# 64-row matmul pairs for the q, k, v products of a gated attention and MLP kernel

## The chip, the cores and the metric

The kernel runs on one core of a Trainium2 chip. The metric is device time in microseconds (us) for one execution of the whole program. A core has TensorE (matrix products, abbreviated PE), VectorE (DVE), ScalarE (ACT), GpSimd (POOL) and SyncE (SP), each with its own queue of instructions that it takes in order; in this kernel SP issues all DMA transfers. Engines wait for one another by semaphores. SBUF is the on-chip memory of 128 partitions ("rows" below). PSUM holds TensorE's results; this kernel uses it as eight tiles of 128 rows by 512 float32, four with the tag "m" and four with the tag "b", handed out in turn within each tag.

## The reference

Two branches read the same x of 2048 positions by 448 features and are mixed by a gate. All matrices are float32.

```
g   = sigmoid(sum(x * gate_w))                       # one number per position
qkv = x @ wqkv                                       # 448 -> 3 x 448, 16 heads of 28
a   = softmax over 8 positions (i, i-2, ... i-14) of q.k / sqrt(28), times v;  then @ wo
b   = relu(x @ w1 + b1)^2 @ w2 + b2                  # 448 -> 1792 -> 448
out = g * a + (1 - g) * b
```

## The kernel before

**Precision.** Every matrix product is made of one-pass products in the type fp32r. Each operand is split: ScalarE writes a rounded copy ("h", high), VectorE writes the rest ("l", low, float32 minus h). A product is then h·h + h·l + l·h. `split_full` (L99) is one such pair of instructions.

**Contraction.** 448 features are three blocks of 128 rows and a last one of 64. A full block takes three matmuls. The last block is stored twice, in rows 0 to 63 and 64 to 127: `x7` holds the high part of x in both halves, `x8` the low part, and `w7` the low part of the weights in rows 0 to 63 and the high part in rows 64 to 127 (`split_w7`, L103), so that two matmuls of 128 rows do it. `pairs` (L132) lists these 3 x 3 + 2 = 11 matmuls of a tile.

**Stage A, the q, k, v products (L447 to L497).** Positions are sorted into even and odd ones, since attention steps by two, and into four chunks c of 512. A chunk has four tiles of 128 positions. Each tile and each of q, k, v (b = 0, 1, 2) is one PSUM tile of 128 positions by 448 features (450 for q, whose last columns are the gate), so there are 4 x 4 x 3 = 48 PSUM tiles of 11 matmuls. Chunk 0 computes q and k with `qkv_wide` (L182), which goes block by block over four tiles because the operands are still arriving, and v tile by tile with `qkv_block` (L175). Chunks 1 to 3 take two tiles at a time: q, q, k, k, v, v, from the tags b, b, m, m, b, b and then m, m, b, b, m, m. ScalarE evacuates each finished tile to a staging tile in SBUF (`qkv_evacuate`, L167), and SP stores it to DRAM (q_d, k_d, v_d; L171), from where attention loads it in another layout.

**What stands between.** While a chunk is computed, the next chunk's x is loaded (`x_load`, L393, 1 MB), split by ScalarE and VectorE, and its split form is written to DRAM (`x_spill`, L128, eight transfers) for stage B. Quarters of w1 and halves of w2 are loaded and split as well (`w1_piece`, L373; `w2_piece`). All of these raw loads share two buffers. At most eight of SP's transfers are under way: each waits for the one eight places before it.

**Order.** The program order is written by hand. A planner keeps a clock of TensorE time: `advance(dt)` (L350) moves it by the cost of the matmuls just issued (`MM448` = 203 ns each), then issues what falls due: work that was put off with `at(dt, fn)`, and the next pieces of attention. The pieces of w1 and w2 are put off by times in `WEIGHTS` (L439), so their ScalarE copies stand between evacuations in ScalarE's queue.

**Attention** starts when the first half of the positions is in DRAM. GpSimd multiplies, VectorE reduces, each in order; it runs on beside the second half of stage A and most of stage B.

**Stage B (L678 to L712)** takes the chunks in the order 3, 0, 1, 2: the MLP, and between its steps the product with wo for the positions that attention has finished. An output tile gets two additions by VectorE, one from each branch (`fin_add`, L572). After the first, the half sum goes to DRAM (f_d, L578); before the second it is loaded again (L552), and the sum goes to `out` (L575). In the last chunk, c = 2 (par = 1, t = 0 to 3), the wo half comes first, and the MLP's half ends the program.

**The start.** Thirteen float32 matmuls of 128 columns on a tile of zeros (L403) run while the first weights and x arrive. The zeros' buffer has the tag "k" of the pool `attp`, and so has the raw copy of the k weights (L416), which is loaded once the warm-up is through with it. Gates are computed after chunks 1 and 3 (`gates`, L268): an exponential on ScalarE, then add, reciprocal and multiply-add on VectorE.

Of the kernel before, what the change touches and what calls it, by code (L numbers as in the profile page):

```python
# [19 lines left out]
G = 4  # L20
# [22 lines left out]
WARM = 13  # L43
PP_BUFS = 4
# [6 lines left out]
def gated_mix_kernel(ctx: ExitStack, tc: tile.TileContext, xT, wqkv, w1, w2, wo, b1, b2, out):  # L51
# [97 lines left out]
    wq7 = ap.tile([P, 3, NQ], F32R, name="wq7")  # L149
# [6 lines left out]
    def qkv_pairs(x, tl, b):  # L156
        n = NQ if b == 0 else D
        sl = slice(tl * P, tl * P + P)
        return n, pairs(lambda k: x.h[k][:, sl], lambda k: x.l[k][:, sl], x.x7[:, sl], x.x8[:, sl],
                        lambda k: wqh[:, k, b, :n], lambda k: wql[:, k, b, :n], wq7[:, b, :n])  # L160

    def qkv_evacuate(pt, c, tl, b):
        par, t = c // 2, (c % 2) * 4 + tl
        if t % 2 == 0:
            stage[b] = ap.tile([P, G, 2, C], F32, tag="stage", name=f"st{c}_{tl}_{b}", bufs=ST_BUFS)
        st = stage[b]
        nc.scalar.activation(st[:, :, t % 2], pt[:, :D].rearrange("p (g c) -> p g c", g=G), AF.Copy)  # L167
        if t % 2 == 1:
            dst, off = ((q_d, 0), (k_d, HALO), (v_d, HALO))[b]
            dd = dst[par, :, off:off + SP].rearrange("g (p s) c -> p g s c", s=NS)[:, :, t - 1:t + 1]  # L170
            nc.sync.dma_start(dd.rearrange("p g s c -> p g (s c)"), st.rearrange("p g s c -> p g (s c)"))  # L171
# [3 lines left out]
    def qkv_block(x, c, tl, b, tag):  # L175
        pt = ps(tag, f"qkv{c}_{tl}_{b}")
        n, pr = qkv_pairs(x, tl, b)
        for i, (a, w) in enumerate(pr):
            nc.tensor.matmul(pt[:, :n], a, w, start=i == 0, stop=i == len(pr) - 1)  # L179
        return lambda: qkv_evacuate(pt, c, tl, b)  # L180

    def qkv_wide(x, c, b, tag):  # L182

        pts = [ps(tag, f"qkv{c}_{tl}_{b}") for tl in range(4)]
        todo = [qkv_pairs(x, tl, b) for tl in range(4)]
        for lo, hi in ((0, 3), (3, 6), (6, 9), (9, 11)):
            for tl in range(4):
                n, pr = todo[tl]
                for i in range(lo, hi):
                    nc.tensor.matmul(pts[tl][:, :n], *pr[i], start=i == 0, stop=i == len(pr) - 1)  # L190
        return [lambda tl=tl: qkv_evacuate(pts[tl], c, tl, b) for tl in range(4)]
# [76 lines left out]
    def gates(par):  # L268
        e = smp.tile([P, NS], F32, tag="e", name=f"e{par}")
        nc.scalar.activation(e, zt[:, par], AF.Exp, scale=-1.0)  # L270
        nc.vector.tensor_scalar_add(e, e, 1.0)
        nc.vector.reciprocal(gt[:, par], e)
        nc.vector.tensor_scalar(g1t[:, par], gt[:, par], -1.0, 1.0, op0=ALU.mult, op1=ALU.add)
# [126 lines left out]
    zero = attp.tile([P, P], F32, tag="k", name="zero")  # L400
    nc.vector.memset(zero, 0.0)  # L401
    for _ in range(WARM):
        nc.tensor.matmul(warm[:, :P], zero, zero, start=True, stop=True)  # L403
# [4 lines left out]
    for k in range(4):  # L408
        nc.sync.dma_start(raws[0][:, k, :NQ], wqkv[0, :, k])
# [3 lines left out]
    raw3 = attp.tile([P, 2, D], F32, tag="q", name="wqraw_3")  # L413
    for b, tag in ((1, "k"), (2, "v")):
        raw = attp.tile([P, 3, D], F32, tag=tag, name=f"wqraw{b}")
        raw = [raw[:, k] for k in range(3)] + [raw3[:, b - 1]]  # L416
        for k in range(4):
            nc.sync.dma_start(raw[k], wqkv[b, :, k, :D])
        raws.append(raw)
    x = x_tiles(0, ap)  # L420
# [9 lines left out]
    split_w7(raws[0][:, 3, :NQ], wq7[:, 0])  # L430
    split_x78(rx[:, 3], x.x7, x.x8)

    def wq_split(b):
        for k in range(3):
            split_full(raws[b][k], wqh[:, k, b, :D], wql[:, k, b, :D])
        split_w7(raws[b][3], wq7[:, b, :D])
# [3 lines left out]
        (0, 8): [lambda: w1_piece(0, 3 * QT)],  # L440
        (1, 2): [lambda: w1_piece(1, 4 * QT)],
        (1, 8): [lambda: w1_piece(2, 3 * QT)],
        (2, 2): [lambda: w1_piece(3, 4 * QT)],
        (2, 8): [lambda: w2_piece(0, 4, w2ah, w2al, 0, 3 * QT)],
        (3, 2): [lambda: w2_piece(4, 3, w2ah, w2al, 0, 4 * QT)],
    }
    for c in range(4):  # L447
        if c == 0:
            order = [(0, None), (1, None)] + [(2, tl) for tl in range(4)]
        else:  # L450
            order = [(b, 2 * tp + i) for tp in range(2) for b in range(3) for i in range(2)]
        done = 0
        for b, tl in order:
            if done == 0 and c < 3:
                rx = x_load(c + 1)
            if done == 0 and c == 0:
                wq_split(1)
            if done == 4 and c == 0:
                wq_split(2)
# [5 lines left out]
            for piece in WEIGHTS.get((c, done), ()):  # L465
                piece()
            if done == (8 if c == 0 else 4) and c < 3:
                xn = x_tiles(c + 1, xpool if c % 2 == 0 else ap)
                x_split(rx, xn)
                if c + 1 < 3:  # L470
                    x_spill(c + 1, xn)
            if done == 4 and c == 0:
                x_spill(0, x)
            if tl is None:
                evs = qkv_wide(x, c, b, "bm"[b])
                for ev in evs:
                    advance(QT)
                    ev()
                done += 4
            else:  # L480
                ev = qkv_block(x, c, tl, b, "bm"[done // 2 % 2])
                advance(QT)
                ev()
# [271 lines left out]
```

## Time and profile before

| | |
|---|---|
| time, median of 3 runs | 442.14 us (441.98 to 446.45) |
| the profiled execution: its time | 442.13 us |
| its span, first to last instruction | 440.4 us |
| TensorE busy | 433.5 us, 2082 records |
| VectorE, ScalarE, GpSimd busy | 260.0, 178.5, 273.6 us |
| granted TensorE clock | 0.999 |
| DMA | 67.44 MB, mean 153 GB/s |
| warm-up matmuls (L403) | 1.06 to 6.69 us |
| q, k, v matmuls (L190, L179) | 6.69 to 114.58 us, 528 of them |

The profile is one execution on the chip. A row of a view in order of time gives the start in us, the duration in us, engine, line, operation, what is written and read, and in brackets how long the engine was idle before and what ended the wait. "PEld" is TensorE's loading of weights, which runs beside the matmuls. A line such as "SPq" is the issue of a transfer by SP's queue, not the transfer. The chain of work that ended last is followed back from the last instruction: at each step to what released it, or to the instruction before it on its engine. In the view by stage each row is a stretch of time: its length, then busy time and count for PE, PEld, DVE, ACT and POOL, then the granted clock, the busy share of the DMA engines and their GB/s.

### The profile page before, as it was taken

How to read it: one execution, taken by the hardware profiler on the slowest of the kernel's cores; microseconds unless marked ns; L12 is line 12 of the kernel's file. 1: busy time of each engine (PE TensorE's matmuls, PEld its weight loads, DVE VectorE, ACT ScalarE, POOL GpSimd, SP SyncE). 2: the span in 40 equal slices, each digit the busy share in tenths (PEclk: the TensorE clock that was granted, in tenths of full speed). 3: DMA queues.
4: the chain of work that ended last, by engine and by line, in shares of the span. 5: the costliest groups of instructions: out<-in, count | busy, mean ns of one | idle time of the engine just before them, and what ended most of it. 6: DMA issues, size and time to landing. Idle time of an engine off the chain costs nothing.

```text
span 440.4 us, 5662 instructions
## 1 busy us (share of the span) xinstructions
PE 433.5 (98%) x2082; PEld 385.8 (88%) x2082; DVE 260.0 (59%) x345; ACT 178.5 (41%) x367; POOL 273.6 (62%) x167
## 2 busy tenths in 40 slices
PE   9999999999999999999999999999999999999994
PEld 8999999999888888888888888888888888888994
DVE  4522411774799996666655857543857757653542
ACT  3644532643455433453334453234233333334520
POOL 1000003574999999999989997641899988690000
PEclk9999999999999999999999999999999999999999
DMA  7899979678560321821203754010544400100145
GB/s 227 323 309 378 384 227 345 238 229 293 172 247 6 136 105 40 309 98 44 78 1 120 237 180 151 34 41 22 173 151 154 173 1 0 78 1 0 64 156 200
DMA packets 37899, 67.44 MB, mean 153 GB/s; under 512 B 3184, under 2 KB 27888, under 8 KB 37488
## 3 DMA queue, kind: packets, MB, share of 16 engines
q1 hardware_dynamic: 37872, 67.08, 44.4%
q8 instruction: 16, 0.26, 0.2%
q14 instruction: 11, 0.09, 0.1%
HBM read 42.38 MB, written 24.69 MB: 152 GB/s over the span
## 4 chain that ended last, share of the span: by engine, by line
PE 97%; DMA 1%; DVE 0%; SPq 0%; DVEq 0%; issue 0%
PE h L533 32%; PE b L594 30%; PE qkv L179 20%; PE a L635 8%; PE qkv L190 4%; PE warm L403 1%; PE oT L612 1%; DMA bt<-f_d 1%; PE oT L613 0%; DVE bt L573 0%; SPq L552 0%; DVEq L750 0%; SPq L575 0%; DVE zero L401 0%; DVEq L573 0%
## 5 line engine op out<-in xcount | busy, mean ns | idle before, releaser
L226 POOL TENSOR_TENSOR qk<-q,k 128x896 f32<-128x896 f32 x64 | 137.8, 2183 | 102.4 <-DMA k<-k_d 71.6
L233 POOL TENSOR_TENSOR av<-lg,v 128x896 f32<-128x896 f32 x64 | 122.8, 2017 | 12.9 <-DVE o L239 6.6
L539 ACT ACTIVATE h<-h,b1t 128x512 f32<-128x512 f32 x56 | 37.1, 662 | 164.1 <-PE h L533 164.0
L179 PE MATMUL qkv<-wqh,x 128*128 128x448 f32 (+1 forms) x240 | 75.0, 367 | 0.0
L542 DVE TENSOR_TENSOR hl<-h,hh 128x512 fp32r<-128x512 f32 x56 | 38.5, 688 | 59.2 <-ACT h L541 59.0
L227 DVE TENSOR_REDUCE lg<-qk 128x32 f32<-128x896 f32 x64 | 67.1, 1076 | 4.0 <-POOL qk L226 4.0
L239 DVE TENSOR_REDUCE o<-av 128x112 f32<-128x896 f32 x64 | 66.7, 1075 | 2.1 <-POOL av L233 2.1
L179 PEld LDWEIGHTS qkv<-wqh,x 128*128 128x128 f32 x240 | 45.2, 188 | 3.8
L179 PE MATMUL qkv<-wql,x 128*128 128x448 f32 (+1 forms) x120 | 44.0, 366 | 0.0
L594 PE MATMUL b<-w2bh,hh 128*128 128x448 f32 x112 | 41.0, 366 | 0.0
L594 PE MATMUL b<-w2bl,hh 128*128 128x448 f32 x112 | 40.9, 366 | 0.0
L594 PE MATMUL b<-w2bh,hl 128*128 128x448 f32 x112 | 40.9, 365 | 0.0
L594 PE MATMUL b<-w2ah,hh 128*128 128x448 f32 x112 | 40.7, 364 | 0.0
L594 PE MATMUL b<-w2ah,hl 128*128 128x448 f32 x112 | 40.6, 362 | 0.0
L594 PE MATMUL b<-w2al,hh 128*128 128x448 f32 x112 | 40.5, 361 | 0.0
L167 ACT ACTIVATE st<-qkv 128x448 f32<-128x448 f32 x48 | 25.4, 547 | 23.3 <-PE qkv L179 17.3
L540 ACT ACTIVATE hh<-h 128x512 fp32r<-128x512 f32 x56 | 33.6, 600 | 1.8
L541 ACT ACTIVATE h<-h 128x512 f32<-128x512 f32 x56 | 33.2, 593 | 0.0
L533 PE MATMUL h<-x1b,w1h 128*128 128x512 f32 x84 | 28.6, 394 | 0.0
L533 PE MATMUL h<-x2b,w1h 128*128 128x512 f32 x84 | 28.5, 393 | 0.0
L533 PE MATMUL h<-x0b,w1h 128*128 128x512 f32 x84 | 28.4, 391 | 0.0
L533 PE MATMUL h<-x,w1h 128*128 128x512 f32 x84 | 28.2, 390 | 0.0
(104 smaller groups left out, 761.2 us busy)
## 6 DMA issues: line engine op xcount, KB each, us to landing
k<-k_d SPq DMA_DIRECT2D x8, 840.0 KB, 5.1
v<-v_d SPq DMA_DIRECT2D x8, 840.0 KB, 5.8
x_d<-x SPq DMA_DIRECT2D x24, 256.0 KB, 4.8
q_d<-st SPq DMA_DIRECT2D x8, 448.0 KB, 4.7
k_d<-st SPq DMA_DIRECT2D x8, 448.0 KB, 4.9
w1raw<-w SPq DMA_DIRECT2D x4, 896.0 KB, 9.1
v_d<-st SPq DMA_DIRECT2D x8, 448.0 KB, 4.4
q<-q_d SPq DMA_DIRECT2D x8, 448.0 KB, 3.4
```

What stands on the lines that cost most here:

```text
L179: nc.tensor.matmul(pt[:, :n], a, w, start=i == 0, stop=i == len(pr) - 1)
L226: nc.gpsimd.tensor_mul(pr, q[:, s:s + 1].to_broadcast([P, W, C]), k[:, s:s + W])
L227: pending.append(lambda: nc.vector.tensor_reduce(lg[:, s], pr.rearrange("p w (h d) -> p w h d", h=HG), axis=AX.X, op=ALU.add))
L233: nc.gpsimd.tensor_mul(pr.rearrange("p (h d) w -> p w h d", h=HG), lg[:, s][:, :, :, None].to_broadcast([P, W, HG, DH]), v[:, s:s + W].rea ...
L239: pending.append(lambda: nc.vector.tensor_reduce(o[:, g * C:(g + 1) * C], pr, axis=AX.X, op=ALU.add))
L533: nc.tensor.matmul(pt, w, a, start=i == 0, stop=i == len(pr) - 1)
L539: nc.scalar.activation(pt, pt, AF.Relu, bias=b1t[:, f:f + 1])
L540: nc.scalar.activation(hh, pt, AF.Square)
L541: nc.scalar.activation(pt, pt, AF.Square)
L542: at(HL_DELAY, lambda: nc.vector.tensor_sub(hl, pt, f32(hh)))
L594: nc.tensor.matmul(bps[tl][:, :D], a[:, sl], w, start=f == 0 and i == 0, stop=f == NF - 1 and i == 2)
L635: nc.tensor.matmul(pa[:, :D], a, w, start=i == 0, stop=i == len(pr) - 1)
```

## The change

**Pairs.** In stage A the contraction is cut into products of 64 rows. A PSUM tile now takes 21 of them: 9 full matmuls as two halves each, and three for the last 64 rows (h·h, h·l, l·h). `side_by_side` issues them in pairs: one product on rows 0 to 63 for one PSUM tile, one on rows 64 to 127 for another. Two tiles thus take 21 pairs instead of 22 matmuls. Each tile gets the products of one half of the rows first, and those of the other half later, beside another tile; the lists in `run`, `qkv_first` and `qkv_two` set this order, and `Acc` keeps count.

**Turns.** Between the two halves `turn` has VectorE write a zero into an unused column of the PSUM tile (ScalarE for two of them in chunk 0). This write waits for the matmuls of the first half, and those of the second wait for it. There are 44 such VectorE writes and 2 on ScalarE. In most cases nine pairs of other tiles are issued between a turn and the matmul that waits for it.

**Chunk 0** keeps 36 full q matmuls (three blocks, four tiles), with 2, 1 and 0 filler matmuls on the zeros after the blocks (`FILL`). Then come 48 pairs, which finish q and make k, and 42 for v. Chunks 1 to 3 have two parts of 63 pairs each, whose tiles have the tags m, m (q), m, b (k), b, b (v). Evacuations are issued at the pair after which a tile is done.

**Weights.** The last 64 rows of q's and k's weights share one tile (rows 0 to 63 and 64 to 127), split into `w7h` and `w7l`; v's stay doubled. One weight load of 224 KB is gone and one is cut into two.

**Order.** The split and the spill of the next x, and the pieces of w1 and w2, are put off to other planner times. The filler matmuls read the zeros too, so the load of the k weights, which takes their buffer, now waits for the last filler.

**Other parts.** Warm-up: fp32r, one pass, 256 columns, 13 matmuls as before. Gates: the addition and the multiply-add move from VectorE to ScalarE. Last output halves: `fin_add` keeps the half sums of par = 1, t < 4 in SBUF, so these four are neither stored to f_d nor loaded again.

The core of the diff:

```diff
+    def side_by_side(*todo):
+        for pair in zip(*todo):
+            for r, (acc, a, w) in enumerate(pair):
+                rows = slice(r * 64, r * 64 + 64)
+                nc.tensor.matmul(acc.pt[:, :acc.n], a[rows], w[rows], start=acc.todo == 21, stop=acc.todo == 1)
+                acc.todo, acc.rows = acc.todo - 1, r
+
+    def turn(one, two):
+        for acc in (one, two) if one is not two else (one,):
+            if one is two:
+                nc.scalar.activation(acc.pt[0:1, 511:512], ident[0:1, 1:2], AF.Copy)
+            else:
+                nc.vector.memset(acc.pt[0:1, 511:512], 0.0)
+            acc.rows = None
...
+    def last(x, acc, tl, b):
+        sl, n = slice(tl * P, tl * P + P), ncols(b)
+        h, l = w7h[:, b // 2, :n], w7l[:, b // 2, :n]
+        return [(acc, x.x7[:, sl], h), (acc, x.x7[:, sl], l), (acc, x.x8[:, sl], h)]
...
+    def run(c, todo, steps):
+        a = 0
+        for e, done, *turns in steps:
+            side_by_side(todo[0][a:e], todo[1][a:e])
+            while a < e:
+                advance(min(12, e - a) * MM448)
+                a = min(a + 12, e)
+            for one, two in turns:
+                turn(one, two)
+            for b, tl, acc in done:
+                qkv_evacuate(acc.pt, c, tl, b)
...
+        for k in range(3):
+            for i in four:
+                for j, (acc, a, w) in enumerate(full(x, q[i], i, 0, (k,))):
+                    nc.tensor.matmul(acc.pt[:, :NQ], a, w, start=k == j == 0, stop=False)
+            advance(12 * MM448)
+            for _ in range(FILL[k]):
+                nc.tensor.matmul(warm[:, :2 * P], zero[:, :P], zero, start=True, stop=True)
...
+    def qkv_two(x, c, t0):
+        t1 = t0 + 1
+        (q0, q1), (k0, k1), (v0, v1) = (accs(c, b, (t0, t1), tags) for b, tags in enumerate(("mm", "mb", "bb")))
+        run(c, [full(x, q0, t0, 0) + last(x, q0, t0, 0) + full(x, q1, t1, 0) + last(x, q1, t1, 0) + full(x, k0, t0, 1)
+                + full(x, k1, t1, 1) + full(x, v0, t0, 2) + last(x, v0, t0, 2) + full(x, v1, t1, 2),
+                full(x, k1, t1, 1) + last(x, k1, t1, 1) + full(x, v0, t0, 2) + full(x, v1, t1, 2) + last(x, v1, t1, 2)
+                + full(x, q0, t0, 0) + full(x, q1, t1, 0) + full(x, k0, t0, 1) + last(x, k0, t0, 1)],
+            [(24, [], (q0, k1)), (33, [], (q1, v0)), (42, [(0, t0, q0), (1, t1, k1)], (k0, v1)),
+             (51, [(0, t1, q1)]), (54, [(2, t0, v0)]), (63, [(1, t0, k0), (2, t1, v1)])])
...
-        nc.vector.tensor_scalar_add(e, e, 1.0)
+        nc.scalar.activation(e, e, AF.Copy, bias=1.0)
         nc.vector.reciprocal(gt[:, par], e)
-        nc.vector.tensor_scalar(g1t[:, par], gt[:, par], -1.0, 1.0, op0=ALU.mult, op1=ALU.add)
+        nc.scalar.activation(g1t[:, par], gt[:, par], AF.Copy, scale=-1.0, bias=1.0)
...
-    zero = attp.tile([P, P], F32, tag="k", name="zero")
+    zero = attp.tile([P, 2 * P], F32R, tag="k", name="zero")
...
-        nc.tensor.matmul(warm[:, :P], zero, zero, start=True, stop=True)
+        nc.tensor.matmul(warm[:, :2 * P], zero[:, :P], zero, start=True, stop=True)
...
+        (0, 2): lambda: w1_piece(0, 3 * QT),
+        (1, 0): lambda: w1_piece(1, 6 * QT),
+        (1, 1): lambda: w1_piece(2, 5 * QT),
+        (2, 0): lambda: w1_piece(3, 6 * QT),
+        (2, 1): lambda: w2_piece(0, 4, w2ah, w2al, 0, 5 * QT),
+        (3, 0): lambda: w2_piece(4, 3, w2ah, w2al, 0, 6 * QT),
...
+                at(4 * QT if c else 8 * QT + 25 * MM448, lambda c=c, rx=rx: x_next(c + 1, rx))
...
+        elif par == 1 and t < 4:
+            ahead[par, t] = bt
+            fin[par, t] = "half"
```

## The prediction

> **What bounds the kernel now.** I read four views in this order: busy time by engine, the chain of work that ended last (its start and, in a second answer, its end: start us, us, what), ScalarE's rows in order of time during the q, k, v products, and the busy time of the engines by stage.
>
> ```profile
> PE 433.5 (98%) x2082; PEld 385.8 (88%) x2082; DVE 260.0 (59%) x345; ACT 178.5 (41%) x367; POOL 273.6 (62%) x167
> ```
> ```profile
> 1.06 5.63 PE warm L403 x26
> 6.69 17.98 PE qkv L190 x88
> 24.67 89.91 PE qkv L179 x440
> ```
> ```profile
> 411.45 0.33 PE oT L612 x3
> 411.77 0.11 PE oT L613
> ...
> 431.81 3.74 DMA bt<-f_d
> ...
> 435.68 0.51 DVE bt L573
> ```
>
> TensorE is busy for 98% and is the chain nearly everywhere, so a matmul less is time less, as long as nothing else ends last. Two reserves show: 5.63 us of warm-up, and the end, where 3.74 us go to reloading a half output. The products fill 6.69 to 114.58 us: 528 matmuls, 107.89 / 528 = 0.2043 us each. The transposes show how fast TensorE goes when the streamed operand is short: 0.11 us for one matmul with its own weight load.
>
> ```profile
> 35.74 0.58 ACT L100 ACTIVATE w1h<-w1raw 128x448 fp32r<-128x448 f32 x1 [6.02 <-DMA w1raw<-w]
> 36.23 0.53 ACT L167 ACTIVATE st<-qkv 128x448 f32<-128x448 f32 x1
> ...
> 79.39 2.20 ACT L100 ACTIVATE x<-xraw 128x512 fp32r<-128x512 f32 x4 [9.19 <-DMA xraw<-xT]
> 81.50 0.52 ACT L167 ACTIVATE st<-qkv 128x448 f32<-128x448 f32 x1
> ```
> ```profile
> 6.70:15.70 9.00, 9.00 (x45) 8.30 (x45) 6.45 (x12) 5.31 (x12) 0.00 (x0) 1.00 1.01 354
> 15.70:24.70 9.00, 9.00 (x45) 8.31 (x45) 2.22 (x4) 3.98 (x11) 0.00 (x0) 1.00 0.74 259
> 24.70:33.70 9.00, 9.00 (x46) 8.32 (x46) 2.50 (x4) 3.69 (x8) 0.00 (x0) 1.00 1.00 329
> 33.70:60.60 26.90, 26.90 (x133) 24.78 (x132) 7.48 (x12) 11.83 (x28) 0.00 (x0) 1.00 1.05 373
> ```
>
> The last two columns are the DMA engines' busy share and GB/s: here they are full. ScalarE takes its work in order, and it twice stands for 6.02 and 9.19 us on a load, with evacuations of finished PSUM tiles (L167) queued behind. TensorE does not notice, because the next tiles it writes are ones emptied long before. That spare decides this change.
>
> **The pairs.** Chunk 0 keeps 36 full-height q matmuls, then has 48 + 42 pairs; chunks 1 to 3 have 126 pairs each. That is 36 + 468 = 504 slots for 528. At 0.2045 us a pair the 24 missing slots are worth 4.9 us.
>
> The trace of before has no 64-row matmul, so the price p of a pair is bounded: 0.2043 us (one full matmul, both halves truly side by side) and 0.409 (no overlap). Between lies 0.22, twice the 0.11 of a matmul with its weight load, if the two loads follow each other. I take 0.2045, as a pair streams the same 448 columns as the row nearest to it in shape. The Trainium skill, page "TensorEngine Tiling (Array Packing)", section "Tiling Modes", says that different tiles can load weights and multiply in parallel. By that rule the sum is the forecast below; by the transposes' row it is the second rival; no run shown here decides.
>
> **The start.** Warm-up becomes 13 one-pass matmuls of 256 columns, priced between 13 x 0.11 = 1.4 and 13 x 0.213 = 2.8 us (5.63 / 26, the present pass), so it ends by 3.9 us, before the first operands (written at 4.1 us). The q matmuls then follow their data, by the ends of VectorE's splits in its rows: the first 12 wait for one at 6.39, the next 12 for one at 8.60, and these with a filler end at 8.60 + 10 x 0.2043 + 0.12 = 10.8. The last 12 need a split that ends at 11.44, about 11.1 without the k loads beside it, which holds only the first of them; they end at 10.8 + 12 x 0.2043 = 13.25 us, against 6.69 + 36 x 0.2043 = 14.05 now. But the k weights land in the buffer that holds the warm-up's zeros, which the three filler matmuls still read: SP issues those loads only after the last filler, at about 10.9 us, where before it was 6.72. Everything on SP's queue behind them moves: v weights, the next x, spills.
>
> **The gap after chunk 0.** 90 pairs from 13.25 would end at 31.65 us (33.66 now). Chunk 1's first pair, however, writes its k half into the bank of chunk 0's first v tile. Its evacuation stands on ScalarE behind the split of the first quarter of w1, as it does now, and that load landed at 35.74 us. Can it land earlier? Its issue comes behind eight spills, two q and two k stores, about 28 us as now (28.22). By volume 9.7 MB land before it is complete; at 354 GB/s, 27.5 us, from 2.0 us, with about 3.3 us empty before the late k weights, it lands at 32.8 at the earliest. With the writes at 329 and the q stores now ahead of it, 37 at the latest. I take 36.0, next to the measured 35.74. Split 0.58 and evacuation 0.53 bring chunk 1 to 37.1 us (33.9 to 38): TensorE stands for about 5.4 us, and chunk 0's gain is gone.
>
> **Chunks 1 to 3.** Chunk 1 takes 126 x 0.2045 = 25.8 and ends at 62.9 us. The v store after it leaves at 64.0 (two evacuations). Before, it left at 65.19 and x for chunk 3 landed 14.2 us later, behind the q, k, v loads of attention; now 78.2. Four conversions (2.20) and three short evacuations (1.1) later, at 81.5, the bank is free that pair 84 of chunk 2 wants at 62.9 + 84 x 0.2045 = 80.1: 1.4 us of wait. The 42 pairs left end at 90.1, chunk 3 at 115.9, where before it was 114.58: **+1.3 us**. In short the end is 55.7 + 294 p.
>
> The 44 memsets on VectorE at 0.17 us (its 128x8 rows at 65 us) are 7.5 us on an engine that is busy 47 of 114.6 us. TensorE waits for each, with nine pairs, 1.84 us, of cover behind most. Queued ahead of them are splits and attention's reduces (1.08 us). At 84 us, in chunk 2, the splits of x end (84.22 before, some 1.2 earlier now) within about half a microsecond of the need; without cover such a turn costs up to 2.4 us, the longest split in that stage. I take nothing and keep 1 us for the range. Behind a memset reduces wait, and GpSimd for them, but attention's products end near 390 us, some 15 before they are wanted.
>
> Two turns and the gates on ScalarE (0.2 us each) lie beside matmuls; the gates are read microseconds later by additions far down the queue, and if ScalarE must wait for the reciprocal it costs one reduce, 1.1 us, under the four spare tiles of the next phase.
>
> **The end.** Four stores and four reloads of 224 KB vanish. Now the last TensorE result is there at 434.6 and the last addition ends at 436.96 (start 435.68, two of them, 1.28). Without the reload the last addition runs 434.6 to 435.3: **-1.7 us**. Late next is the addition itself and the output store, about 2 us, as now. Held tiles could starve the pool of nine; at most eight are in use, so nothing.
>
> **Sum.** 442.13 + 1.3 - 1.7 = **441.7 us**. The profiled execution took 442.13 (span 440.4 and 1.7 around it), the median is 442.14, so no correction. About 1%, 4.4 us, is what a measurement of this kernel tells from no change.
>
> **Rivals.**
> 1. *The load is no obstacle.* If it lands by 30.5, or the bank is empty in time, the products end at 31.65 + 378 x 0.2045 = 108.95: -5.6 and -1.7 give 434.8. For it: 98% busy TensorE and a chain without any DMA in this stage. Against it: 35.74 measured, full DMA engines, and k weights asked for 4 us later. Chance 0.24.
> 2. *Weight loads pace the pairs, slower than before.* The place is every pair, the price 0.22, and the side turns at p = 0.206, where 55.7 + 294 p - 1.7 reaches 114.58. At 0.22 the products end at 120.4, hence 446.2. For it: PEld is busy 88%, each load record 0.19 us, and a pair has two. Against it: these loads lie beside the matmul now. Chance 0.24.
> 3. *The halves do not run side by side.* 0.409 for 468 pairs ends the products at 204.7: about 530 us; the change would not do what it says. The trace has no two matmuls that start together. Chance 0.13.
> 4. *TensorE comes back slow from its gap.* No idle time over 1.1 us is in this trace and the granted clock is 0.999, so nothing shows what 5 us do. If it runs at half pace for as long as the present warm-up, 5.63 us, it costs 2.8: 444.3. The Trainium skill, page "TensorE: Matmul & The Clock Gate", section "Part 1: The HAM clock gate", says that an idle window of about 3.4 us halves the rate until a busy one has passed; an estimate by that figure is 1.7 us, 443.2, and no run here shows it. Chance 0.07.
>
> The forecast, 441.7, keeps 0.32, with 439 to 443.5 as its own range (landing between its bounds, one late turn).
>
> **The numbers.** The likeliest is the forecast. The range leaves out rival 3 and the far edges: 433.5 (rival 1, 1.3 us to spare for a pair a little under 0.2043) to 449 (rival 2 with late turns). Faster by over 1%, below 437.7: rival 1 and a little of the forecast, 0.27. Slower, above 446.5: rival 3, half of rival 2 and a late-turn remainder, 0.28. Between: 0.45.
>
> **What will show it.** Right: pairs 0.20 to 0.21 apart; TensorE idle some 5 us near 32 us, ended by ScalarE's evacuation behind the w1 split; a second stop near 80 us; k weights issued at 11 us; no DMA in the chain at the end. Wrong: no idle TensorE between 31 and 38 us, or pairs at another pace. If the w1 load lands by 31 us, the step on volumes was wrong.

## The result and the profile after

The changed kernel takes 447.92 us, median of 6 runs (447.19 to 448.81), against 442.03 us for the kernel before in the same rounds: a ratio of 1.0118, 95% interval 1.008 to 1.0155. It is slower by 1.2%. The forecast was 441.7 us, the time before to within 1%. The profiled execution took 447.19 us with a span of 445.4 us.

The first view is the page's busy times and its granted clock in 40 slices of 11.1 us.

```profile
PE 430.9 (97%) x2516; PEld 384.5 (86%) x2516; DVE 263.1 (59%) x384; ACT 178.4 (40%) x372; POOL 273.7 (61%) x167
...
PEclk9996999999999999999999999999999999999999
```

TensorE is busy for 2.6 us less than before, and the span is 5.0 us longer: TensorE has stood still for longer than it has saved. The clock has one dent, in the fourth slice, which before was not there. The second view lists what TensorE waited for: us in total, times, longest.

```profile
PE qkv L176 <- ACT st L195: 8.6, 2, 7.1
...
PE qkv L176 <- ACT qkv L184: 0.4, 1, 0.4
```

Two waits for evacuations (L195), 8.6 us together; before, TensorE waited for nothing in the products. Not one wait is for VectorE's turns (L186); the 0.4 us is for one of the two turns on ScalarE (L184). The chain of waits carries, in this stretch, the loads that answer to the two waits (start us, us, what):

```profile
32.05 6.79 DMA w1raw<-w
39.92 27.62 PE qkv L176 x248
68.58 4.05 DMA v_d<-st
73.07 9.92 DMA xraw<-xT
86.19 34.82 PE qkv L176 x318
121.00 7.71 PE h L610 x33
```

The products end at 121.00 us; before, at 114.58. That is +6.4 us. From there to the end of the span it is 324.4 us instead of 325.8, so 1.4 us come back, and 6.4 - 1.4 is the 5.0 us of the two spans. ScalarE's rows show the two places where its queue stood on a load, and one more:

```profile
29.34 1.42 ACT L195 ACTIVATE st<-qkv 128x448 f32<-128x448 f32 x3 [6.56 <-DMA q_d<-st]
...
38.86 0.58 ACT L101 ACTIVATE w1h<-w1raw 128x448 fp32r<-128x448 f32 x1 [6.03 <-DMA w1raw<-w]
39.34 1.82 ACT L195 ACTIVATE st<-qkv 128x448 f32<-128x448 f32 x4
...
83.02 2.19 ACT L101 ACTIVATE x<-xraw 128x512 fp32r<-128x512 f32 x4 [5.82 <-DMA xraw<-xT]
```

And TensorE's busy time by stage, with granted clock, busy share of the DMA engines and GB/s in the last three columns:

```profile
6.70:15.70 9.00, 8.93 (x57) 7.68 (x55) 5.57 (x10) 2.94 (x5) 0.00 (x0) 1.00 0.65 185
15.70:24.70 9.00, 8.61 (x86) 7.65 (x84) 3.04 (x9) 5.07 (x16) 0.00 (x0) 1.00 0.95 339
24.70:32.80 8.10, 8.10 (x79) 7.11 (x75) 1.68 (x7) 3.46 (x7) 0.00 (x0) 1.00 0.87 300
32.80:39.92 7.12, 0.00 (x0) 0.00 (x1) 1.45 (x3) 1.09 (x4) 0.00 (x0) 0.77 0.99 293
39.92:43.60 3.68, 3.68 (x20) 3.35 (x22) 1.34 (x3) 2.65 (x6) 0.00 (x0) 0.52 1.05 401
43.60:52.60 9.00, 9.00 (x92) 8.81 (x90) 1.42 (x8) 2.15 (x6) 0.00 (x0) 1.00 0.84 310
```

Four things are to be seen. From 6.70 to 15.70 us the DMA engines move 185 GB/s, where before they moved 354: the hole that the late k weights leave. From 32.80 to 39.92 us TensorE does nothing. In the 3.68 us after that its clock is 0.52, with 20 records where the next stretch has about 10 a microsecond (a record is half a pair). And then the pairs run at full speed, 0.204 to 0.206 us apart from row to row.

### The profile page after: what moved, and what is told of

Its sections match the earlier page's. It is cut to its first block, busy times and chain, and to the rows that moved or that the text cites. A ratio compares the mean times of both kernels' runs of the same rounds, so it can differ in the third digit from the quotient of the medians.

```text
span 445.4 us, 6597 instructions
## 1 busy us (share of the span) xinstructions
PE 430.9 (97%) x2516; PEld 384.5 (86%) x2516; DVE 263.1 (59%) x384; ACT 178.4 (40%) x372; POOL 273.7 (61%) x167
## 4 chain that ended last, share of the span: by engine, by line
PE 86%; DMA 8%; SPq 2%; ACT 1%; issue 1%; DVE 0%; ACTq 0%
PE h L610 32%; PE b L674 30%; PE qkv L176 14%; PE a L715 8%; DMA xraw<-xT 5%; DMA w1raw<-w 2%; PE oT L692 1%; DMA v_d<-st 1%; DMA q_d<-st 1%; SPq L131 1%; ACT st L195 1%; ACT x L101 1%; SPq L504 1%; PE qkv L244 1%; PE oT L693 0%
## 5 line engine op out<-in xcount | busy, mean ns | idle before, releaser
L176 PE MATMUL qkv<-wqh,x 64*128 64x448 f32 (+1 forms) x528 | 90.6, 369 | 9.0 <-ACT st L195 8.6
L176 PEld LDWEIGHTS qkv<-wqh,x 64*128 64x128 f32 x528 | 70.1, 188 | 12.7 <-ACT st L195 9.4
L176 PE MATMUL qkv<-wql,x 64*128 64x448 f32 (+1 forms) x264 | 68.0, 369 | 0.0
L195 ACT ACTIVATE st<-qkv 128x448 f32<-128x448 f32 x48 | 24.1, 544 | 49.0 <-PE qkv L176 42.4
L176 PEld LDWEIGHTS qkv<-wql,x 64*128 64x128 f32 x264 | 40.8, 188 | 1.0
```

Of the source, the lines that this page charges most:

```text
L176: nc.tensor.matmul(acc.pt[:, :acc.n], a[rows], w[rows], start=acc.todo == 21, stop=acc.todo == 1)
```

## The experiments

e4, e9 and e12 start from the kernel before, the others from the changed one. Medians, the ratio to the kernel before in the same rounds, and the end of the q, k, v products in the profiled execution:

| kernel | median us | ratio (95%) | products end, us |
|---|---|---|---|
| changed | 447.92 | 1.0118 (1.008 to 1.0155) | 121.0 |
| e1, w1 split later | 454.42 | 1.0249 (1.0193 to 1.0304) | 128.6 |
| e2, q stores ahead of spills | 448.05 | 1.0113 (1.0056 to 1.0169) | 120.6 |
| e3, TensorE kept busy in the gap | 447.81 | 1.0111 (1.0046 to 1.0175) | 121.8 |
| e4, before + output halves | 441.49 | 0.999 (0.9946 to 1.0034) | 114.3 |
| e5, zeros elsewhere | 444.53 | 1.0044 (1.0029 to 1.0059) | 118.4 |
| e6, w1 load ahead of spills | 449.25 | 1.0156 (1.0139 to 1.0173) | 123.4 |
| e7, all loads ahead of spills | 446.31 | 1.0086 (1.0069 to 1.0103) | 120.8 |
| e8, and x of chunk 3 early | 447.40 | 1.0117 (1.0101 to 1.0134) | 120.2 |
| e9, before + halves + warm-up | 440.43 | 0.9965 (0.9924 to 1.0006) | 115.5 |
| e10, stream arranged | 439.41 | 0.989 (0.9813 to 0.9968) | 110.7 |
| e12, before + all but the pairs | 439.99 | 0.9946 (0.9925 to 0.9967) | 114.5 |
| e13, stream arranged, second form | 438.96 | 0.9911 (0.9879 to 0.9942) | 112.5 |

### e1: the split of w1 behind the evacuations

```diff
-        (0, 2): lambda: w1_piece(0, 3 * QT),
+        (0, 2): lambda: w1_piece(0, 5 * QT),
```

> One number is changed: the split of the first quarter of w1 is put off by 5 QT instead of 3 QT, so that on ScalarE it stands behind the four v evacuations of chunk 0; the load itself is issued as before. Theory A (TensorE stood 7.12 us only because those evacuations wait behind a copy that waits for the load): the copies of the next x end at 32.8 us, the first v evacuation at 33.4, so chunk 1 starts at about 33.4 instead of 39.92, the gap is at most 1 us, and with it goes the half clock of 3.6 us (1.7 us). Products end at 121.0 - 6.5 - 1.7 = 112.8 us, the kernel takes about 439.7 us, 0.982 of the changed kernel. Rival B (the full DMA queues hold this stage whatever the order on ScalarE): the stop moves to the next thing that needs ScalarE, which now stands on the load inside chunk 1, and the products end within 2 us of 121; the kernel stays at 446 to 448.

The gap after chunk 0 is gone, as theory A said: chunk 1 starts at 33.60 us. But the products end 7.6 us later than in the changed kernel. TensorE's rows in which it had waited over 2 us:

```profile
53.78 0.47 PE L176 MATMUL qkv<-wqh,x 64*128 64x448 f32 x1 [2.68 <-ACT st L195]
61.90 0.74 PE L176 MATMUL qkv<-wqh,x 64*128 64x448 f32 x2 [5.41 <-DVE qkv L186]
91.46 0.74 PE L176 MATMUL qkv<-wqh,x 64*128 64x448 f32 x1 [3.38 <-ACT st L195]
```

ScalarE now stands on the w1 load, then on a staging tile whose store is late, and then, at 50.61 us, on x of chunk 2, with the evacuations of chunk 1 behind each. At 61.90 us it is a turn: VectorE had it queued behind the split of the second w1 quarter, which landed at 60.5 us (it was asked for at 53.80 us, where the changed kernel asks at 44.90). So the place of the first wait was found rightly, and rival B is right on the kind: the stop moves to the next instruction that waits for the stream of transfers. The size is neither's: 454.42 us is worse than the 446 to 448 of rival B, since the stops add up to more and the clock halves after two of them.

### e2: is it the issue of the load, or the volume ahead of it?

The row at 29.34 us above suggests why the load of w1 was asked for so late, at 32.05 us: the k evacuations waited 6.56 us for a staging tile, held by a q store that stood on SP behind eight spills. This kernel lets the q stores pass.

```diff
-                x_spill(0, x)
+                at(14 * MM448, lambda x=x: x_spill(0, x))
```

> The eight spills of chunk 0's x are issued 14 planner slots later, so that SP's queue takes the two q stores ahead of them instead of behind them; the order on ScalarE is that of the changed kernel. Theory A (the load of w1 came 2.8 us later than the prediction took it because the k evacuations waited for a staging tile that the q store, queued behind the spills, gave back only at 29.24 us): q stores leave at about 18 us, k evacuations run at about 24.5 instead of 29.3, the load of w1 is issued at about 28 instead of 32.05 and lands at 34 to 36 instead of 38.84, the gap is 3 to 4.5 us, the products end about 3 to 4 us earlier and the kernel takes 444 to 445 us. Rival B (the landing is set by the volume on full DMA queues, not by when it is asked for): it lands at 38 to 39 again, the gap stays near 7 us and the time near 447.9.

The first part came as theory A expected: the load is issued at 28.79 us. It lands at the same time as ever. SP's row and ScalarE's:

```profile
28.79 1.30 SPq L460 DMA_DIRECT2D w1raw<-w  x1
```
```profile
38.70 0.58 ACT L101 ACTIVATE w1h<-w1raw 128x448 fp32r<-128x448 f32 x1 [10.80 <-DMA w1raw<-w]
```

38.7 us against 38.86, a gap of 6.68 against 7.12 us, 448.05 us. Asking earlier does not by itself bring the load earlier: here the DMA engines are full from 30.10 to 38.68 us (their busy share is 1.01), and the spills behind the load share them with it. By the landing 11.0 MB had moved (285 GB/s over 38.68 us), in the changed kernel 10.1 MB (260 GB/s over 38.84 us). Theory A, formed on the trace alone, fell.

### e3: the clock after the gap

```diff
+        if c == 1 and t0 == 0:
+            for _ in range(34):
+                nc.tensor.matmul(q0.pt[:, :NQ], x.h[0][0:64, 0:P], wqh[0:64, 0, 0, :NQ], start=True, stop=True)
         run(c, [full(x, q0, t0, 0) + last(x, q0, t0, 0) + ...
```

> The changed kernel with 34 extra matmuls of 64 rows and 450 columns ahead of chunk 1, written to the PSUM tile of its first q tile, which the real products then start anew; they need nothing that chunk 1 waits for, and fill most of the gap of 7.12 us (34 x 0.2045 = 6.95 us). Their result is thrown away. Theory A (TensorE comes back from the idle gap at half its clock for about 3.6 us): with TensorE busy the first pairs of chunk 1 are 0.20 us apart instead of 0.37, the granted clock stays near 1.0, the products end about 1.7 us earlier and the kernel takes about 446.2 us. Rival (the slow pairs come from something else at that place, such as the write of the first w1 split or the transfers): pairs stay 0.37 apart for 3.6 us and the time stays at 447.9, or a little over.

By stage, the gap and the 3.7 us after it:

```profile
32.80:40.20 7.40, 7.24 (x37) 6.21 (x34) 1.73 (x4) 1.37 (x4) 0.00 (x0) 1.00 1.00 301
40.20:43.90 3.70, 3.69 (x36) 3.63 (x38) 1.91 (x6) 2.65 (x6) 0.00 (x0) 1.00 1.05 400
```

The clock stays at 1.00, and in 3.70 us there are 36 records where there were 20 in 3.68. So the slow pairs came from TensorE's idle time and nothing else at that place. Yet the time is 447.81 us, the same. Chunk 1 ends earlier, and then TensorE stands longer for the next transfers: 1.67 us at 85.07 for x of chunk 3, and 1.36 us at 101.99 for a turn that VectorE had behind splits of w2 and reduces of attention. What is won ahead of a late transfer is given back at it.

### e5: the hole at the start of the stream

```diff
-    zero = attp.tile([P, 2 * P], F32R, tag="k", name="zero")
+    zero = attp.tile([P, 2 * P], F32R, tag="q", name="zero")
```

> The changed kernel with one word changed: the warm-up's zeros lie in the buffer with the tag q instead of k, so the loads of the k weights no longer wait for the last filler matmul at 10.9 us; they should leave at about 6.7 us as in the kernel before. Fillers and order are kept. Theory A (the transfers of the first 40 us are one full stream, and the hole of about 4 us at its start moved the landing of the first w1 quarter): it lands at 34.8 to 35.5 instead of 38.84, the gap is 3 to 4 us, the products end about 3.9 us earlier and the kernel takes about 443.5 us, 1.004 of before. Rival B (the landing is held by something else in the stream, the spills' turn at the limit of eight or the stores; the hole is hidden): it stays at 38 to 39 and the time at 447 to 448.

One letter gives 3.4 us. The k weights are asked for at 5.9 us, the DMA engines move 355 GB/s from 6.70 to 15.70 us, and ScalarE and TensorE show the rest:

```profile
35.66 0.58 ACT L101 ACTIVATE w1h<-w1raw 128x448 fp32r<-128x448 f32 x1 [6.85 <-DMA w1raw<-w]
```
```profile
36.72 0.74 PE L176 MATMUL qkv<-wqh,x 64*128 64x448 f32 x1 [4.12 <-ACT st L195]
```

The load lands where it landed in the kernel before (35.74 us). Theory A holds in kind: the hole moved the landing. Closing it also brings the asking forward, from 32.05 to 27.28 us, but e2 shows that the asking alone does nothing. Its sizes were a little too good: 444.53 us where it said about 443.5, a gap of 4.12 us where it said 3 to 4. The clock still halves after the gap (0.74 is the duration of a slow matmul in these rows), and for longer: 0.52 from 36.72 to 41.90 us.

### e6, e7, e8: the same transfers in another order

e6 moves the spills of chunk 0's x behind the load of w1. e7 adds e5's edit and puts chunk 1's spills off by 4 QT; e8 also loads x of chunk 3 in the second half of chunk 1.

```diff
             WEIGHTS.get((c, i), lambda: None)()
+            if c == 0 and i == 2:        # e6, e7, e8; no spill in part 1
+                x_spill(0, x)
...
+        if c == 1:                       # e7, e8
+            at(4 * QT, lambda x=xs[c]: x_spill(1, x))
...
+            if c == 1 and i == 1:        # e8
+                early[3] = x_load(3)
```

> The changed kernel with the eight spills of chunk 0's x (2 MB) moved behind the load of the first w1 quarter; the order on ScalarE and the late k weights are kept. Theory A (the gap after chunk 0 is the volume ahead of that load): 2 MB at about 340 GB/s are 6 us, so it lands at 31 to 33 us and chunk 1 starts at about 33.5 with a gap of at most 1 us and the full clock. The spills then stand ahead of the next x instead, which landed at 50.5 and stays there by volume: its copies hold the remaining evacuations of chunk 1's first half, and TensorE waits 2 to 3 us near 50 us. Products end near 117 us, 442 to 443.5 us in all. Rival B (nothing is late next): products end at 112.8 us, 439.7 us. Rival C (the load does not come earlier): 447.9.

> The two edits above together, and the spills of chunk 1's x also behind the load of chunk 2's x and of the second w1 quarter: all that TensorE waits for is ahead of the spills on SP's queue, and the hole at the start is closed. Theory A (transfers' order and the hole are all that took the gain in chunks 0 and 1): no TensorE gap over 1 us before chunk 2, products of chunk 1 end at 32.0 + 25.8 = 58 to 59 us; only the wait for x of chunk 3, of which the load stands behind attention's, is left, 1.5 us as in the changed kernel. Products end near 111 us, the kernel takes 437 to 438 us, 0.99 of before. Rival B (the stream as a whole is too slow, whatever its order): gaps of 3 us or more come back later, products end at 114 or later and the time is 441 or more.

> As the previous kernel, and the load of x for chunk 3 is issued in the second half of chunk 1, ahead of the third w1 quarter and of attention's loads. Theory A (that load, 14 us behind the v store, is the cause of the stop near 86 us): no TensorE gap there either, products end at 109 to 110 us, the kernel takes about 436 us, 0.986 of before. Rival B (the third w1 quarter or attention's loads are late in its place): a wait of 1.5 us or more near the end of chunk 1 or in chunk 2, and 437.5 us or more.

None gave what theory A wanted. In e6 the load came 3.5 us earlier (35.4), not 6. It was asked for at 27.36 us, after 2.66 us in which the DMA engines were busy for 0.41 only, and then shared them with the spills that follow it at once (0.99 from 30.00 to 35.36 us). A gap of 3.33 us was left. The x of chunk 3 then kept its old time, 82.9 us, and TensorE stood 4.37 us for it instead of 1.47. In e7 the gap after chunk 0 shrinks to 1.46 us, in e8 to 1.48. But SP now had 16 spills in a row from 38 to 54 us, and the stores of chunk 1 behind them, so staging tiles came back late. One ScalarE row of e7, and one TensorE row of e8:

```profile
59.72 0.55 ACT L195 ACTIVATE st<-qkv 128x448 f32<-128x448 f32 x1 [9.46 <-DMA q_d<-st]
```
```profile
70.86 0.74 PE L176 MATMUL qkv<-wqh,x 64*128 64x448 f32 x2 [4.49 <-DVE qkv L186]
```

9.46 us of ScalarE for a q store; and 4.49 us of TensorE for a turn, which VectorE had behind the reciprocal of the gates and the splits of the third w1 quarter; ScalarE, which feeds both, stood on that quarter until 66.81 us. In e8 there is no wait for x of chunk 3 any more, so that part of its theory A is right, and the wait went where rival B put it. The prediction's 1 us for late turns holds in the changed kernel, where VectorE's turns cost nothing, and not in every order of the transfers.

### e10 and e13: the stream arranged for the faster products

```diff
-        (0, 2): lambda: w1_piece(0, 3 * QT),
+        (0, 1): lambda: w1_piece(0, 7.4 * QT),      # load 48 pairs earlier, split where it was
-        (1, 1): lambda: w1_piece(2, 5 * QT),
-        (2, 0): lambda: w1_piece(3, 6 * QT),
+        (1, 1): lambda: w1_piece(2, 7 * QT),
+        (2, 0): lambda: w1_piece(3, 8 * QT),         # e13: 10 * QT
...
+        if c == 1:
+            at(4 * QT, lambda x=xs[c]: x_spill(1, x))   # e13: 6 * QT
...
+            if (c, i) in ((0, 2), (3, 0)):               # spills of chunk 0, and of chunk 2 in chunk 3
+                x_spill(c - c // 3, x if c == 0 else x2)
```

(With e5's edit, e8's load, and the w2 splits 2 QT later.)

> The changed kernel with the transfers arranged for the faster products: zeros in the q buffer; the first w1 quarter is loaded 48 pairs earlier, ahead of the q and k stores; the spills of x for chunks 0, 1 and 2 are put behind that load, behind the load of chunk 2's x, and into chunk 3; x of chunk 3 is loaded in the second half of chunk 1; the later w1 and w2 splits stand 2 QT later. Nothing is left out. Theory A (the pairs gain what they should, 24 slots or 4.9 us, and all that took it away is evacuations, staging tiles and turns queued behind copies and stores that wait for transfers): no TensorE gap over 1 us in the products, which end at 32 + 378 x 0.2045 = 109.3 us, the clock stays at 1.0, and the kernel takes about 435.5 us, 0.985 of before. Rival B (the stream cannot feed products of 0.2045 us a pair in any order): gaps of 3 us or more in all, products end at 112.5 or later, 438.5 us or more.

> The changed kernel with the arranged transfers of e10, and two more moves: the spills of chunk 1's x stand 6 instead of 4 QT into chunk 1, behind the stores of its first half, and the split of the last w1 quarter 10 instead of 8 QT into chunk 2. Theory A (pairs gain 4.9 us in TensorE's slots, and e10's executions between 438 and 444 were evacuations and turns that just missed their transfers): products end at 109.3 to 110 us, 435 to 437 us in all, 3 to 5 us under e12, and less spread than e10. Rival B (the gain of the arranged version is that of tail, warm-up and gates): within 1 us of e12, about 439.5.

In e10's profiled execution (span 435.1 us) TensorE waits for one turn, 0.6 us, and for nothing else after the warm-up. Its waits and chain:

```profile
PE qkv L176 <- DVE qkv L186: 0.6, 1, 0.6
```
```profile
13.80 52.97 PE qkv L176 x512
...
82.25 28.44 PE qkv L176 x272
110.69 7.70 PE h L614 x33
```

The products end at 110.7 us, against 109.3 expected and 121.0 in the changed kernel: the stream can feed pairs of 0.2045 us, in this order. But only one execution of four was as fast as that (436.87 us; the median is 439.41, and 438.53 without the execution at 443.78, which the ratio leaves out). Rival B is refuted by the trace, while the median lies in its range of times. e13 is steadier (437.13 to 439.34) and not clearly faster: two turns, behind splits and reduces on VectorE, hold TensorE for 1.46 and 0.77 us, and the products end at 112.5. Both versions are faster than the kernel before by about 1%, with intervals below 1.

### e11: what a pair costs when its stream is short

```diff
-                nc.tensor.matmul(acc.pt[:, :acc.n], a[rows], w[rows], start=..., stop=...)
+                n = acc.n if acc.todo == 21 else 128
+                nc.tensor.matmul(acc.pt[:, :n], a[rows], w[rows, :n], start=..., stop=...)
```

> The changed kernel in which each half of a pair but the first of a tile's sum streams 128 columns instead of 448 or 450, so that the rest of these columns lacks its later products; it measures what a pair costs when the stream is short. If the two halves load their weights side by side, pairs within an uninterrupted run are 0.06 us (128 / 448 of 0.2045) to 0.11 us apart (the transposes' full matmul of 128 columns in the trace of before). If they load one after the other, they are 0.18 to 0.22 us apart, and at 448 columns the loads are only just hidden.

TensorE's rows (a row of x4 is two pairs), and its clock by stage:

```profile
17.83 0.39 PE L177 MATMUL qkv<-wqh,x 64*128 64x128 f32 x4
18.05 0.28 PE L177 MATMUL qkv<-wql,x 64*128 64x128 f32 x2
18.16 0.39 PE L177 MATMUL qkv<-wqh,x 64*128 64x128 f32 x4
```
```profile
16.80:18.60 1.80, 1.80 (x36) 1.80 (x36) 0.40 (x3) 1.80 (x10) 0.00 (x0) 1.00 1.02 268
18.80:31.50 12.70, 12.70 (x120) 12.61 (x120) 2.51 (x10) 2.14 (x5) 0.00 (x0) 0.50 0.89 325
60.00:80.00 20.00, 20.00 (x185) 20.00 (x185) 4.10 (x18) 5.44 (x15) 0.00 (x0) 0.50 0.84 279
```

Two pairs in 0.22 us: 0.11 us a pair, the price of one full matmul with a short stream. The two halves load their weights side by side. Then, two microseconds after a stop of 1.33 us that ended at 16.55, TensorE falls to half clock at about 18.6 us. It stays there to 31.5 us without a single wait, and is there at 60 to 80 us. A pair then takes 0.22 us (185 records in 20.00 us), more than a pair of 448 columns at full clock, and the kernel, of the least streaming, takes 454.9 us in its one execution.

### e4, e9, e12: the other parts, alone

e4 is the kernel before with the last output halves kept in SBUF, e9 adds the one-pass warm-up, e12 the gates on ScalarE. Their diffs are the change's own.

> The kernel before with one part of the change alone: the half sums of the last four output tiles stay in SBUF. Theory A: the chain's end without the reload is 1.4 to 1.7 us shorter (the difference between the two traces from the end of the products to the end, and the prediction's sum), so about 440.5 us. Rival: the shorter end in the changed kernel comes from its other parts, and this one alone gives 0 to 0.5 us: 441.6 to 442.

> The kernel before with two parts of the change: the last output halves kept in SBUF and the one-pass warm-up of 256 columns; products stay full height, 528 matmuls. Theory A: the warm-up ends by 3.9 us, the first 36 products follow their data and end near 13.25 us instead of 14.05 (0.8 us), the tail gives 1.6 us: about 439.6 us, 0.9945 of before. Rival B (without the fillers of the changed kernel the products start at a low clock, or the earlier chunk 0 runs into the load of w1): 441 us or more.

> The kernel before with every part of the change but the pairs: last output halves kept, one-pass warm-up, gates on ScalarE. Theory A (the addition of the gates on VectorE takes as long as GpSimd holds it off, 1.6 to 6.9 us in three traces where 0.17 was measured with GpSimd idle, and when long it stops TensorE for 2.7 us and slows its clock): without it the executions at 444 to 446 us, 4 of 10 in the same kernel with gates on VectorE, are gone, and nearly all lie at 439.5 to 441 us; median about 440.0. Rival B (the two levels come from something else, such as where the loads of the next stage fall): 3 or 4 of 10 are still above 444.

e4's tail is as the prediction had it: from the start of the last long run of MLP matmuls to the end of the span, 94.95 us against 96.66 before, so 1.7 us. But the median moved by 0.8 us only, because four of its ten executions took 444.8 to 445.5 us and six 439.7 to 442.1. The profiled one is of the upper group, and shows why. VectorE's row, TensorE's, and TensorE's clock after its stop:

```profile
115.00 6.87 DVE L271 TENSOR_SCALAR e<-e 128x8 f32<-128x8 f32 x1 [1.08 <-ACT e L270]
```
```profile
124.95 0.64 PE L597 MATMUL b<-w2ah,hl 128*128 128x448 f32 x1 [2.74 <-DVE hl L542]
```
```profile
125.00:128.50 3.50, 3.50 (x10) 3.15 (x11) 3.47 (x5) 0.00 (x0) 2.96 (x4) 0.51 0.55 150
```

An addition of 128 x 8 numbers for the gates took 6.87 us; the same line took 0.17 us at 64.97 us, before GpSimd's work begins. In three traces the second addition took 1.62, 6.87 and 1.92 us. In e4 GpSimd multiplied without a break from 112.26 to 121.84 us, and the addition ended at 121.87. In the two others (before and e9) it ended within 0.03 us of the end of one GpSimd instruction. The MLP's low parts wait behind it on VectorE, TensorE stands 2.74 us, and half a clock for 3.5 us costs about 1.75 more: 4.5 us, about the distance of the two groups. The Trainium skill, page "SBUF — State Buffer", section "SBUF: two separate sides", says that GpSimd and some operations of VectorE share a pair of ports as an exclusive lock, held for a whole instruction, and that the loser blocks. The trace agrees, and the loser here waited for four GpSimd instructions, not one.

e12 has the gates on ScalarE: ten executions of ten at 439.6 to 440.5 us, median 439.99. Three of ten were above 444 in e9, which differs from it by the gates alone (the expectation named e4's four). That is what theory A said, but it is weak evidence: in e12's rounds, on another chip, the kernel before, with the gates on VectorE, was above 444 in only one execution of 15, against 3 of 13 both in the rounds of e4 and in those of e9. So the mechanism is shown in the one execution of e4 that was traced; that the gates' move removes the upper group is likely and not shown. The prediction priced the move at nothing.

The 0.8 us expected of the warm-up is not seen: e9's products ended at 115.5 us in its profile, e12's at 114.5, against 114.6 before. In e9 the first products are 0.37 to 0.38 us apart until about 10 us, where before they are 0.20 apart, and the 36th ends 0.9 us later than before. Its rival B had named a low clock at that place; the granted clock reads 1.00 there, so the cause of the slow pace is not shown. In e12, with the same start, the slow pace ends at about 6.3 us, in the changed kernel at about 6.0.

e13 against e12 is the worth of the pairs with an arranged stream: 438.96 against 439.99 us, 1.0 us. It is small but there: the slowest of e13's six executions, 439.34 us, is faster than the fastest of e12's ten, 439.62, in the same rounds. In the profiles the products end 2.0 us earlier. Theory A of e13 (435 to 437 us) is missed, and rival B (within 1 us of e12) is missed by less than 0.1 us. An arranged stream with full matmuls was not run; but e12's TensorE waits for nothing in its products, so there was nothing for the order of transfers to win there. Of the 4.9 us of missing slots, e10's profile shows that most can be had (110.7 against 114.5), the medians that they mostly are not.

## Why the prediction was wrong, and where it was right

**Bound and pairs: right.** A pair takes 0.2045 us from row to row, and 0.206 on average with its turns over e10's 468 pairs, (110.69 - 13.80 - 0.64) / 468. The rule of the Trainium skill, page "TensorEngine Tiling (Array Packing)", section "Tiling Modes", that tiles load and multiply in parallel, agrees with this and with 0.11 us at 128 columns in e11. So rivals 2 (0.22) and 3 (0.409) fall.

**The start: right in its times, the warm-up not.** The q matmuls ended at 13.2 us (13.25 predicted), and the k weights were asked for at 10.95 (10.9). The warm-up took 3.14 us, above its bounds of 1.4 to 2.8, and ended at 4.34 instead of 3.9; its cost did not show, since the next twelve q matmuls wait for their data until 8.50 us, as predicted (8.60).

**The gap after chunk 0: right mechanism, wrong size. This is the step that failed:** "I take 36.0, next to the measured 35.74", with 32.8 to 37 as bounds. The load landed at 38.84 us. The prediction had moved the whole stream by the 4.2 us between 6.72 and 10.95 us in its step on the start, and then took nearly the landing of the kernel before, by rates (354 and 329 GB/s) of stretches that were full; the row at 15.70 us, with 0.74 and 259, is not full, though the text calls the rows so. Its sum by volume counted 9.7 MB and 3.3 us empty. Measured, 260 GB/s over 38.84 us are 10.1 MB, and the 9.0 us at 185 instead of 354 GB/s are a loss of 9.0 x (354 - 185) / 354 = 4.3 us. e5, which closes the hole, lands at 35.64: the hole is what moved it. The load was also asked for at 32.05 us and not at about 28, but e2, where it is asked for at 28.79, lands at 38.70. Chunk 1 thus began at 39.92 us instead of 37.1.

**The clock: rival 4, put beside the forecast where it belonged inside it.** With a stop of 5 us in the forecast, its consequence for the clock was a term of the sum, not a case of 0.07. It cost 20 records in 3.68 us where 36 would fit, some 1.7 us; the forecast's sum had it at nothing. e3 shows the cause. The price is not fixed: after 4.49 us of stop in e8 the clock was at 0.50 for 6.00 us, which costs 3.0. The estimate of 1.7 us that the prediction made from the Trainium skill, page "TensorE: Matmul & The Clock Gate", section "Part 1: The HAM clock gate", fits this case, with some luck. Rival 4's totals are 0.2 us too low: 441.7 + 2.8 is 444.5, and 441.7 + 1.7 is 443.4.

**Chunk 2's wait and chunk 3: right in size.** The x of chunk 3 was converted 14.4 us after the v store (14.2 predicted), and TensorE stood 1.47 us (1.4). All of it came later by what the gap had cost.

**Turns: right here, not in general.** No turn on VectorE held TensorE in the changed kernel, and the 44 writes took 0.06 us each, not 0.17; one of the two on ScalarE, which were taken to cost nothing, held it for 0.4 us. In e1, e3, e7, e8 and e13 VectorE's turns held TensorE for 5.41, 1.36, 2.08, 4.49 and 1.46 us at a time. The cover of nine pairs, 1.84 us, does not protect against a VectorE whose next split waits for a transfer (e1, e7, e8), nor against one that is simply full: ahead of the turns of e3 and e13 it had worked without a break from 95.01 to 101.85 and from 83.17 to 93.7 us, with splits that took up to 1.9 us there and 0.62 elsewhere.

**The tail: right.** 1.6 us by the last long run of matmuls (95.05 against 96.66), 1.7 predicted; 0.2 us of it were lost between the products and that run. Of the gates see e12.

**The sum.** Predicted end of products 115.9, measured 121.0: 2.8 from the landing, 1.8 from chunk 1 (27.62 us instead of 25.8, nearly all of it the clock), 0.1 from the wait in chunk 2, and 0.4 from the last 168 pairs, which took 34.8 us instead of 34.4. With the tail, 442.13 + 6.4 - 1.4 = 447.1, measured 447.19. The range, 433.5 to 449, held the time because rivals on both sides were in it, not because this case was: the forecast's own range, 439 to 443.5, did not hold it.

**What stays open.** It is open what makes the arranged versions' spread, 436.87 to 443.78 in e10: only one execution of each was traced. It is open, too, why the half clock lasts about 3.5 us after one stop and 6.0 after another, and whether the upper group of e4 and e9 always has the cause that was traced once. No kernel was tried in which the turns stand on an engine that has nothing else in its queue.

## What to carry to other kernels

An engine that is busy 98% of the time can still be fed by a stream with no reserve: before shortening its work, ask by what time each transfer must land after the change, and move every landing by what the change does to the queue in front of it. When the stream is full, reordering one transfer moves the stop to the next instruction that stands in an in-order queue behind a transfer, be it an evacuation, a store or a one-element write; here only an order for the whole stage (e10, e13) made the change pay. And a gap of some microseconds on TensorE is to be priced at its length plus the clock that it costs, here 1.7 to 3.0 us more.

## What was not expected of the hardware

- **How short a stop costs the clock, and for how long.** 2.74 us of idle time on TensorE in e4 were followed by 3.5 us at 0.51, 3.23 us in e7 by 5.57 us at 0.50, and 4.49 us in e8 by 6.00 us at 0.50; after 3.33 us in e6 the first 1.06 us were at 0.99 and the next 3.40 at 0.50. 2.08 us in e7 and 2.68 in e1 left the clock at 1.00. No run shows that a fixed length is the edge. The Trainium skill, page "TensorE: Matmul & The Clock Gate", section "Part 1: The HAM clock gate", speaks of an idle window of about 3.4 us; the traces differ, since stops of 2.74, 3.23 and 3.33 us were enough here.
- **A full queue need not bring the clock back.** In e11 TensorE waited for nothing from 18.8 to 31.5 us and ran at 0.50 throughout, with matmuls of 64 rows and 128 columns. In the other kernels it was back at 1.00 within 6.3 us after every stop. What holds it down in e11 is not shown.
- **A tiny VectorE instruction beside GpSimd.** The same addition took 0.17 us before GpSimd's work began and 6.87 us beside it in e4, and TensorE stopped for it.
